# State products in parts of 64 rows and whole 128x128 scores for chunks 0 to 8 of a linear attention with a feed-forward layer

## The chip, the core and the metric

The kernel runs on one core of a Trainium2 chip. The core has a matrix engine (TensorE, in the profile PE, its weight loads PEld), a vector engine (VectorE, DVE), a scalar engine (ScalarE, ACT), a general engine (GpSimd, POOL) and SyncE (SP), which here issues all DMA transfers between the main memory and the on-chip memory (SBUF). TensorE writes its results to PSUM, from which the other engines read. The metric is the device time of one execution in microseconds (us); the figure given for a kernel is the median of several runs.

## The reference

A recurrence with a state of 48x48 for each of 4 batches and 8 heads runs over 768 time steps; its output goes through a token mixing of rank 32 and a feed-forward layer of 384 to 1536 to 384 channels, all in fp32.

```python
def _attn_ref(r, k, v, w, u):
    state = np.zeros((B, H, D, D))
    for t in range(S):
        cur = np.einsum('bhd,bhe->bhde', u[None] * kt, vt)
        y[:, :, t] = np.einsum('bhd,bhde->bhe', rt, state + cur)
        state = wt[:, :, :, None] * state + np.einsum('bhd,bhe->bhde', kt, vt)

def _moe_ref(x, U, V, w_ch1, w_ch2):
    h = x.transpose(0, 2, 1) @ U @ V
    u = x + h.transpose(0, 2, 1)
    return u + np.maximum(u @ w_ch1, 0.0) @ w_ch2
```

## The kernel before

The recurrence is cut into 24 chunks of 128 time steps, six for each batch; chunk g belongs to batch g // 6. Heads stand in pairs: pair j (0 to 3) has its even head in partitions 0 to 47 and its odd head in partitions 64 to 111. Within a chunk the recurrence becomes matrix products. VectorE scans the decays (`scan_f`, L393, and `scan_q`, L408); r and k are scaled by the scans (L416, L421, L423). Then the chunk has these steps on PE:

- the scores (`scores`, L560, step AM): products of scaled k and scaled r over the 48 channels of a head, written to the PSUM tile `aps` of 128 x 2 x 4 x 128. Only k at or before r in time matters. The keys are cut into two halves of 64, and each head's product is made in parts of 64 output rows: one half of the keys meets all 128 times of r, the other only the last 64. The quarter that stays out was set to zero once, at the start (L236). For pairs 2 and 3 the halves of the keys stand in swapped order;
- the u products (`rows_by_u`, L499, step MD, chunks 0 to 5): the diagonal of the scores;
- the transposition of k (`turn_k`, L525, step KT, chunks 0 to 8), which ScalarE copies to the SBUF tile `kn` (`copy_k`, L545, step KN). For chunks 9 to 23 (`TURN_K_DVE`) VectorE and DMA transfers transpose k in blocks of 32 instead;
- the state products (`state_add`, L577 and L578, step DS): kn times v, written to the PSUM tile `dS` in parts of 32 rows. For chunks 1 to 4 (`ADD_Z_PE`) PE also adds the old state Z with a product by the identity matrix (L577) in front of each; for the others VectorE adds it (L608). The last chunk of a batch has no state products;
- y (`y_inner`, L637 and L647, step YA; `y_state`, L660 and L664, step YZ): the scores, merged with the diagonal, times v, and r times the state. Both write parts of 32 rows.

VectorE merges the scores into the tile A that holds the diagonal (`merge`, L567, step CP): a mask says which elements are taken from `aps`. ScalarE makes the next state Z from `dS` (`decay`, L617) and copies y (`out_x`, L681). Behind the chunks come the token mixing and, in seven blocks of time, the feed-forward layer (`ffn`: L888 up, L922 down), whose weights are split into a high and a low half first (L305 to L342).

The order of the work on every engine is written out: the string `ORDER` lists all steps, and `plan` runs them in that order. An engine takes its instructions in that order, and each waits by semaphores for what it reads and for the buffers it writes. SP's queue of transfers is one such list too. [rows N] means the group **Rows N.** below.

Of the kernel before, what the change touches and what calls it, by code (L numbers as in the profile page):

```python
# [13 lines left out]
AF = mybir.ActivationFunctionType  # L14
# [5 lines left out]
B, H, S, D = 4, 8, 768, 48  # L20
P = 128
NP = H // 2
# [14 lines left out]
HP = P // 2  # L37
# [5 lines left out]
TURN_K_DVE, TURN_X_DVE = [9, 10, 11, 12, 13, 14, 15, 16, 17, 18, 19, 20, 21, 22, 23], [9, 10, 11, 12, 13, 14, 15, 16, 17, 18, 19, 20, 21, 22, 23]  # L43
CHOICES = 3
DIAG_PE, LATE_GUARD = [0, 1, 2, 3, 4, 5], []
DIAG_V, MIX_AT_ONCE, X_PE, UP_PARTS = [], [], [], []
LOW_PE = dict(w1=[], w2=[], V=[])
ADD_Z_PE = (1, 2, 3, 4)
W_MAX, W_MAX_BITS, DECAY_MIN = 1.25, 0x3FA00000, 1e-16
HIGH_MIN, HIGH_END = 1.125 * 2.0**-15, 122880.0  # L50
# [108 lines left out]
def rwkv_moe_kernel(ctx, tc, wT, rkT, vN, vS, rkN, uB, uT, uD, U, V, w1, w2, out):  # L159
    nc = tc.nc  # L160
# [18 lines left out]
    def place(kind, shape, name, buf=None, dtype=F32):  # L179

        n = buf.slot if buf else None
        if n is None:
            n = turns[kind] % slots[kind]
            turns[kind] += 1
        return homes.get(kind, sb2).tile(shape, dtype, tag=f"{kind}{n}", name=name)
# [11 lines left out]
    def warm(n, to):  # L197
        for _ in range(n):
            nc.tensor.matmul(to, busy[:, 0:P], busy[:, 0 : to.shape[1]], start=True, stop=True)

    def lead(to):
        if leading[0]:
            warm(leading[0], (to.rearrange("p a b -> p (a b)") if len(to.shape) == 3 else to)[:, 0:TB])

    warm(8, idle)
    ident = const.tile([P, P], F32, name="ident")
# [30 lines left out]
    dS = psS.tile([P, NP, ZW], F32, name="dS")  # L237
# [7 lines left out]
    def step(name, eng, fn, after=(), take=(), use=(), alt=None):  # L245

        s = Step(name, eng, fn, after, list(take), list(use), alt.split() if alt else None)
        steps.append(s)
        return s
# [100 lines left out]
    def chunk(g):  # L350
        b, c = divmod(g, NCH)
        st = sts[g] = dict(buf={p: Buf(p) for p in ("w", "v", "F", "Q", "dv", "kn", "Z", "aps", "y", "dS", "qd")})
        st["buf"].update((p, Buf("big")) for p in ("rk", "kr", "A"))
        buf = st["buf"]
        old = sts.get(g - 1) if c > 0 else None
# [80 lines left out]
        f = step("F " + nm, "DVE", scan_f, [lw], take=[buf["F"]], use=[buf["w"]])  # L436
# [7 lines left out]
        q = step("Q " + nm, "DVE", scan_q, [rc], take=[buf["Q"]], use=[buf["w"], buf["qd"]])  # L444
# [96 lines left out]
                )  # L541

        def copy_k():
            st["kn"] = place("kn", [P, 4, NP, 32], f"kn_{g}", buf["kn"])
            nc.scalar.activation(  # L545
                st["kn"].rearrange("p q j c -> p j q c"), st["trk"].rearrange("p j (q c) -> p j q c", c=32), AF.Copy
            )

        def scores():
            rk = st["rk"]  # L550
            aps = st["aps"] = aps_all
            lead(aps[:, 0])
            for j in range(NQ):
                for h in range(2):
                    for i in range(2):
                        r = slice(64 * i, 64 * i + D)
                        for a in range(2):
                            jj, s0 = j + NQ * (a ^ h), HP * h
                            k0 = HP * a
                            nc.tensor.matmul(  # L560
                                aps[HP * a : HP * a + HP, i, jj, s0:P], rk[r, 1, jj, k0 : k0 + HP], rk[r, 0, jj, s0:P],
                                start=True, stop=True,
                            )
# [4 lines left out]

        def state_add():
            kn, v = st["kn"], st["v"]  # L570
            for j in range(NP):
                for q in range(4):
                    i = q // 2
                    r = slice(32 * q, 32 * q + 32)
                    to = dS[r, j, i * D : i * D + D]
                    if z_pe:
                        nc.tensor.matmul(to, ident[:, r], old["Z"][:, j, i * D : i * D + D], start=True, stop=False)  # L577
                    nc.tensor.matmul(to, kn[:, q, j, :], v[:, j, 64 * i : 64 * i + D], start=not z_pe, stop=True)  # L578

        on = c < NCH - 1  # L580
        z_pe = g in ADD_Z_PE
        if on:
            if g in TURN_K_DVE:
                btk = Buf("big")
                kn = step("KB " + nm, "DVE", turn_k_blocks, [ks], take=[btk], use=[buf["rk"]])
                kn = step("KW " + nm, "SP", send_k, [kn], use=[btk])
                kn = step("KL " + nm, "SP", fetch_k, [kn], take=[buf["kn"]])
            else:
                btr = Buf("ffn")
                kt = step("KT " + nm, "PE", turn_k, [ks], take=[btr], use=[buf["rk"]])  # L590
                kn = step("KN " + nm, "ACT", copy_k, [kt], take=[buf["kn"]], use=[btr])
        am = step("AM " + nm, "PE", scores, [rp, ks], take=[buf["aps"]], use=[buf["rk"]])
        cp = step("CP " + nm, "DVE", merge, [am] + sel_, use=[buf["aps"], buf["A"]])
        if on:
            ds = step(
                "DS " + nm, "PE", state_add, [kn, lv] + ([old["z"]] if z_pe else []), take=[buf["dS"]],
                use=[buf["kn"], buf["v"]] + ([old["buf"]["Z"]] if z_pe else []),
            )
# [651 lines left out]
```

## Time and profile before

| | us |
|---|---|
| median of three runs | 430.25 (428.70 to 431.21) |
| the profiled execution | 429.46 |
| its span, first to last instruction | 427.8 |

Busy time in the span: PE 411.3 us (96%, 4518 matmuls), PEld 359.0 us, DVE 296.6 us (69%), ACT 173.3 us (41%), POOL 121.9 us (28%). The chain that ended last is PE for 82%, 69% of the span in the feed-forward's two lines (35% L922, 34% L888); the scores are 3% of it and the state products 1%. A line of the profile names an engine, a line of the kernel and an operation with its output and inputs; "48*64 48x128" at a matmul means that 48 rows and 64 columns of the array are used and 128 columns move through it (where products of two widths follow each other, the line shows the first). A matmul of fp32 stands as two instructions in the trace.

### The profile page before, as it was taken

To read this page: it belongs to the slowest core of one execution; us is meant where nothing else is said; L and a number is where in the kernel's file an instruction comes from. 1 tells how busy PE (TensorE), PEld (TensorE's weight loads), DVE (VectorE), ACT (ScalarE), POOL (GpSimd) and SP (SyncE) were. 2 spreads that over 40 slices of the span, in tenths; PEclk is the share of its full clock that TensorE was granted. 3 is DMA by queue.
4 is the path that set the end of the run, shared out by engine and by line. 5 is a ranking of instruction groups with operands and counts; after the bars stand their busy time and mean duration, and the time that the engine had idled before them with its cause. 6 is when DMAs were issued, how large, how long until landed. Compare 5 with 4: busy or idle time off the path is not lost.

```text
span 427.8 us, 11110 instructions
## 1 busy us (share of the span) xinstructions
PE 411.3 (96%) x4518; PEld 359.0 (84%) x4518; DVE 296.6 (69%) x585; ACT 173.3 (41%) x499; POOL 121.9 (28%) x164
## 2 busy tenths in 40 slices
PE   6997899999999999999999999999999999999994
PEld 4986668899999898888878888888787899999984
DVE  8999999999879787978749894185851545115610
ACT  5989987768553317645031110351231102100300
POOL 5654656555774530250300201250000010000000
PEclk8569999999999999999999999999999999999998
DMA  8989772476768797656774611425535011001011
GB/s 281 313 289 295 252 272 97 159 227 211 269 221 279 220 302 281 183 170 211 207 231 147 186 58 51 113 89 188 147 103 177 0 61 38 18 5 64 2 38 43
DMA packets 42874, 69.51 MB, mean 163 GB/s; under 512 B 12224, under 2 KB 25280, under 8 KB 42816
## 3 DMA queue, kind: packets, MB, share of 16 engines
q1 hardware_dynamic: 42816, 68.74, 49.9%
q8 instruction: 37, 0.61, 0.6%
q14 instruction: 21, 0.17, 0.1%
HBM read 57.91 MB, written 10.81 MB: 161 GB/s over the span
## 4 chain that ended last, share of the span: by engine, by line
PE 82%; DVE 5%; issue 1%; ACT 0%; POOL 0%; DVEq 0%
PE f L922 35%; PE f L888 34%; PE aps L560 3%; PE y L637 2%; PE y L647 2%; PE y L660 2%; PE dS L578 1%; PE hp L839 1%; PE y L664 1%; PE ga L785 1%; DVE cva_w L318 1%; DVE cva_w L305 1%; PE gb L796 1%; DVE F L393 0%; DVE w1l L342 0%
## 5 line engine op out<-in xcount | busy, mean ns | idle before, releaser
L888 PE MATMUL f<-u,w1h 128*128 128x384 f32 (+1 forms) x504 | 146.8, 363 | 1.0 <-POOL u L855 0.5
L922 PE MATMUL f<-hid,w2h 128*128 128x384 f32 (+1 forms) x504 | 145.8, 363 | 0.9 <-DVE flag L1148 0.9
L888 PEld LDWEIGHTS f<-u,w1h 128*128 128x128 f32 x504 | 92.8, 188 | 12.4 <-issue 1.2
L922 PEld LDWEIGHTS f<-hid,w2h 128*128 128x128 f32 x504 | 92.8, 188 | 10.7 <-issue 2.0
L922 PE MATMUL f<-hid,w2l 128*128 128x384 f32 (+1 forms) x252 | 90.7, 360 | 0.0
L888 PE MATMUL f<-u,w1l 128*128 128x384 f32 (+1 forms) x252 | 90.7, 360 | 0.0
L893 ACT ACTIVATE hid<-f 128x384 fp32r<-128x384 f32 (+1 forms) x50 | 25.9, 527 | 104.8 <-PE f L888 101.8
L899 DVE SCALAR_TENSOR_TENSOR hid<-f,hid 128x384 fp32r<-128x384 f32 (+1 forms) x84 | 50.5, 610 | 23.0 <-ACT hid L893 22.2
L922 PEld LDWEIGHTS f<-hid,w2l 128*128 128x128 f32 x252 | 47.4, 188 | 4.7
L888 PEld LDWEIGHTS f<-u,w1l 128*128 128x128 f32 x252 | 47.4, 188 | 4.1
L472 ACT ACTIVATE A<-ident,dv 128x128 f32<-128x128 f32 x140 | 43.8, 391 | 14.1 <-DVE dv L458 14.0
L940 DVE TENSOR_TENSOR xT<-f,xT 128x384 f32<-128x384 f32 (+1 forms) x21 | 12.6, 607 | 44.0 <-PE f L922 44.0
L855 POOL TENSOR_TENSOR u<-xT,u 128x384 fp32r<-128x384 f32 (+1 forms) x11 | 12.3, 1132 | 90.7 <-DVE u L851 51.9
L567 DVE COPY_PREDICATED A<-maskf,aps 128x1024 f32<-128x1024 uint32 x24 | 31.6, 1315 | 8.4 <-POOL A L478 5.0
L325 POOL TENSOR_TENSOR cva_w<-cva_w,raw_w 128x384 int32<-128x384 int32 x24 | 25.4, 1071 | 36.9 <-ACT raw_w L312 7.2
L408 DVE TENSOR_TENSOR_SCAN Q<-w,starts,qd 128x258 f32<-128x258 f32 x48 | 33.3, 734 | 2.7 <-POOL rk L416 2.2
L416 POOL TENSOR_TENSOR rk<-rk,Q 128x512 f32<-128x512 f32 x15 | 17.9, 1195 | 56.7 <-DVE Q L408 30.7
L393 DVE TENSOR_TENSOR_SCAN F<-w,qd 128x259 f32<-128x259 f32 x48 | 30.4, 676 | 1.3 <-DMA w<-in_wT 1.3
L895 DVE TENSOR_SCALAR hid<-f 128x512 fp32r<-128x512 f32 (+1 forms) x34 | 21.2, 622 | 10.5 <-PE f L888 10.4
L560 PE MATMUL aps<-rk 48*64 48x128 f32 (+1 forms) x768 | 23.5, 265 | 1.4 <-POOL rk L416 1.4
L560 PEld LDWEIGHTS aps<-rk 48*64 48x64 f32 x768 | 20.1, 144 | 5.6 <-issue 2.5
L849 ACT ACTIVATE u<-xT 128x384 fp32r<-128x384 f32 (+1 forms) x15 | 8.1, 563 | 34.8 <-PE f L922 26.0
(126 smaller groups left out, 522.6 us busy)
## 6 DMA issues: line engine op xcount, KB each, us to landing
raw_w<-in_w SPq DMA_DIRECT2D x48, 384.0 KB, 4.6
rk<-in_rkT SPq DMA_DIRECT2D x24, 512.0 KB, 5.5
kr<-in_rkN SPq DMA_DIRECT2D x18, 384.0 KB, 3.8
w<-in_wT SPq DMA_DIRECT2D x24, 260.0 KB, 4.3
v<-in_vS SPq DMA_DIRECT2D x24, 224.0 KB, 4.2
kd<-kt SPq DMA_DIRECT2D x12, 256.0 KB, 3.0
kn<-kd SPq DMA_DIRECT2D x48, 64.0 KB, 3.0
out_dram<-xT SPq DMA_DIRECT2D x12, 192.0 KB, 2.4
```

The source lines that it names most:

```text
L325: lambda: nc.gpsimd.tensor_tensor(out=d["to"].bitcast(I32), in0=d["a"].bitcast(I32), in1=d["e"], op=ALU.add),
L393: nc.vector.tensor_tensor_scan(out=back(F), data0=back(st["w"]), data1=back(qd, OVER * h), initial=1.0, op0=ALU.mult, op1=ALU.add)
L408: nc.vector.tensor_tensor_scan(out=st["Q"][:, a:e], data0=st["w"][:, a:e], data1=qd[:, a - OVER * h : e - OVER * h], initial=starts[:, h : ...
L416: ENG[eng].tensor_tensor(out=rk[:, 0], in0=rk[:, 0], in1=Qv, op=ALU.mult)
L472: nc.scalar.activation(to, one, AF.Copy, scale=dv[:, NP * i + j : NP * i + j + 1])
L560: nc.tensor.matmul(aps[HP * a : HP * a + HP, i, jj, s0:P], rk[r, 1, jj, k0 : k0 + HP], rk[r, 0, jj, s0:P], start=True, stop=True,)
L567: nc.vector.copy_predicated(to, mask2, new)
L888: nc.tensor.matmul(ps, wt[:, f, ct, :], u[ct][:, z], start=(m == 0), stop=(m == 8))
L893: nc.scalar.activation(h[:, 0], d["ps", f], AF.Relu)
L895: nc.vector.tensor_scalar(out=h[:, 0], in0=d["ps", f], scalar1=0.0, scalar2=None, op0=ALU.max)
L899: nc.vector.scalar_tensor_tensor(out=h[:, 1], in0=d["ps", f], scalar=0.0, in1=h[:, 0].bitcast(F32), op0=ALU.max, op1=ALU.subtract)
L922: nc.tensor.matmul(d["o", ct], wt[:, 4 * ct + part, f - 3 * part, :], hid[f][:, z], start=(part == 0 and m == 0), stop=(part == 3 and m == 8),
```

## The change

For chunks 0 to 8 the scores of a head are one product with all 128 keys and all 128 times, so that the masked quarter is computed too; the mask of the merge keeps it out of A. For the same chunks `kn` keeps the layout of the transposition, 128 keys in one piece for each pair, and the state products are made in parts of 64 rows. Where PE adds the old state, the identity products of a pair now all stand in front of its products with v. The steps and their order are the same. Chunks 9 to 23 keep parts of 32 rows and scores in 64 x 128 and 64 x 64.

```diff
+WHOLE_SCORES = range(9)
...
         def copy_k():
-            st["kn"] = place("kn", [P, 4, NP, 32], f"kn_{g}", buf["kn"])
-            nc.scalar.activation(
-                st["kn"].rearrange("p q j c -> p j q c"), st["trk"].rearrange("p j (q c) -> p j q c", c=32), AF.Copy
-            )
+            st["kn"] = place("kn", [P, NP, P], f"kn_{g}", buf["kn"])
+            nc.scalar.activation(st["kn"], st["trk"], AF.Copy)
...
             lead(aps[:, 0])
+            if g in WHOLE_SCORES:
+                for j in range(NP):
+                    for i in range(2):
+                        r = slice(64 * i, 64 * i + D)
+                        nc.tensor.matmul(aps[:, i, j], rk[r, 1, j], rk[r, 0, j], start=True, stop=True)
+                return
...
         def state_add():
             kn, v = st["kn"], st["v"]
+            m = 32 if g in TURN_K_DVE else HP
             for j in range(NP):
-                for q in range(4):
-                    i = q // 2
-                    r = slice(32 * q, 32 * q + 32)
-                    to = dS[r, j, i * D : i * D + D]
-                    if z_pe:
-                        nc.tensor.matmul(to, ident[:, r], old["Z"][:, j, i * D : i * D + D], start=True, stop=False)
-                    nc.tensor.matmul(to, kn[:, q, j, :], v[:, j, 64 * i : 64 * i + D], start=not z_pe, stop=True)
+                parts = [(slice(q, q + m), slice(q // HP * D, q // HP * D + D), q) for q in range(0, P, m)]
+                for r, cs, q in parts if z_pe else ():
+                    nc.tensor.matmul(dS[r, j, cs], ident[:, r], old["Z"][:, j, cs], start=True, stop=False)
+                for r, cs, q in parts:
+                    kq = kn[:, q // 32, j, :] if m == 32 else kn[:, j, r]
+                    vq = v[:, j, 64 * (q // HP) : 64 * (q // HP) + D]
+                    nc.tensor.matmul(dS[r, j, cs], kq, vq, start=not z_pe, stop=True)
```

The rows below list PE's instructions at two places, by line, operation, output, inputs and shape of the output; a number behind a name tells one tile from another, and x8 stands for eight alike. First PE before the change at chunk 8: its state products, its scores, and the token mixing's product behind them.

```order
L578 MATMUL dS<-v_1429,kn_1426 32x48 x16
L560 MATMUL aps<-rk_1023 64x128 x4
L560 MATMUL aps<-rk_1023 64x64 x4
L560 MATMUL aps<-rk_1023 64x128 x4
L560 MATMUL aps<-rk_1023 64x64 x4
L839 MATMUL hp_1_1506<-Vst,gs_1101 128x384
```

The same place on PE after the change (the lines moved by six).

```order
L584 MATMUL dS<-v_1277,kn_1274 64x48 x8
L556 MATMUL aps<-rk_895 128x128 x8
L845 MATMUL hp_1_1338<-Vst,gs_973 128x384
```

Sixteen state products became eight of twice the rows, and sixteen scores of 64 rows became eight of 128 rows, all 128 columns wide; what stands in front and behind is the same.

The second place is PE at the state products of chunk 7 with y of chunk 7 and the transposition of k of chunk 8 behind them, before the change.

```order
L578 MATMUL dS<-v_1055,kn_1227 32x48 x16
L637 MATMUL y_1386<-A_1205,v_1055 32x128 x8
L647 MATMUL y_1386<-A_1205,v_1055 32x128 x8
L660 MATMUL y_1386<-rk_697,Z_1268 32x128 x8
L664 MATMUL y_1386<-rk_697,Z_1268 32x128 x4
L525 MATMUL trk_1415<-ident,rk_1023 128x128 x4
```

And after it.

```order
L584 MATMUL dS<-v_927,kn_1083 64x48 x8
L643 MATMUL y_1234<-A_1061,v_927 32x128 x8
L653 MATMUL y_1234<-A_1061,v_927 32x128 x8
L666 MATMUL y_1234<-rk_625,Z_1124 32x128 x8
L670 MATMUL y_1234<-rk_625,Z_1124 32x128 x4
L526 MATMUL trk_1263<-ident,rk_895 128x128 x4
```

Before, the state products and y had parts of 32 rows alike; now parts of 32 rows follow parts of 64. The products of y are the same.

## Rows read from the trace of the kernel before

**Rows 1.** Stretches: us; busy PE, PEld, DVE, ACT, POOL; PEclk; DMA; GB/s.

```profile
8.10:28.60 20.50, 19.43 (x313) 17.93 (x316) 19.50 (x43) 17.64 (x58) 14.83 (x18) 0.50 0.95 311
28.60:66.30 37.70, 31.80 (x757) 25.36 (x749) 36.33 (x75) 34.12 (x102) 21.31 (x23) 1.00 0.75 260
66.30:100.40 34.10, 33.94 (x374) 31.92 (x374) 33.34 (x70) 25.14 (x70) 19.22 (x20) 1.00 0.54 171
100.40:406.80 306.40, 306.40 (x2985) 267.49 (x2984) 199.07 (x377) 92.70 (x264) 62.46 (x94) 1.00 0.46 146
```

**Rows 2.** Waits of PE from 60 us on: releaser; us in total, times, longest.

```profile
PE f L922 <- DVE flag L1148: 0.9, 1, 0.9
PE f L888 <- POOL u L855: 0.5, 1, 0.5
PE f L888 <- DVE hid L899: 0.3, 1, 0.3
```

**Rows 3.** Chain that ended last, 65.5 to 75 us: start, us, what.

```profile
66.33 6.51 PE f L888 x36
```

**Rows 4.** PE by time, 72 to 80.5 us: start, us, engine, line, count.

```profile
72.78 0.55 PE L578 MATMUL dS<-v,kn 128*32 128x48 f32 x32
73.14 0.62 PE L637 MATMUL y<-A,v 128*32 128x128 f32 x16
73.58 0.62 PE L647 MATMUL y<-A,v 128*32 128x128 f32 x16
...
78.82 0.55 PE L578 MATMUL dS<-v,kn 128*32 128x48 f32 x32
79.29 0.90 PE L560 MATMUL aps<-rk 48*64 48x128 f32 x32
80.12 0.44 PE L839 MATMUL hp<-Vst,gs 96*128 96x384 f32 x1
```

**Rows 5.** PE by time, 35 us: u products of chunk 5, next instruction.

```profile
35.35 0.95 PE L499 MATMUL trd<-u_diag,kr 128*128 128x2 f32 x8
36.23 0.27 PE L577 MATMUL dS<-Z,ident 128*32 128x48 f32 x5
```

**Rows 6.** PE by time, 8 to 12 us: chunk 0.

```profile
8.60 1.56 PE L560 MATMUL aps<-rk 48*64 48x128 f32 x32 [0.95 <-POOL rk L416]
10.09 1.86 PE L499 MATMUL trd<-u_diag,kr 128*128 128x2 f32 x8
11.81 0.45 PE L525 MATMUL trk<-ident,rk 128*128 128x128 f32 x1
```

**Rows 7.** PE by time, 22 to 31 us: chunk 1, u products.

```profile
24.60 0.29 PE L578 MATMUL dS<-v,kn 128*32 128x48 f32 x1 [0.56 <-DMA v<-in_vS]
...
25.73 0.41 PE L637 MATMUL y<-A,v 128*32 128x128 f32 x1
...
28.87 1.05 PE L499 MATMUL trd<-u_diag,kr 128*128 128x2 f32 x8
```

**Rows 8.** PE by time, 38 to 45 us: state products of chunk 4.

```profile
43.32 0.30 PE L577 MATMUL dS<-Z,ident 128*32 128x48 f32 x7 [2.87 <-ACT Z L617]
...
44.24 0.55 PE L754 MATMUL trx<-ident,xT 128*128 128x128 f32 x3
```

**Rows 9.** ScalarE by time, 28 to 31 us.

```profile
29.49 0.48 ACT L681 ACTIVATE xT<-y 128x384 f32<-128x384 f32 x1
```

**Rows 10.** Waits of VectorE, 4 to 66.3 us.

```profile
DVE F L393 <- DMA w<-in_wT: 1.3, 3, 0.5
DVE Q L408 <- POOL rk L416: 0.9, 1, 0.9
```

**Rows 11.** VectorE by time, 25 to 27 us: merge of chunk 2.

```profile
25.49 1.33 DVE L567 COPY_PREDICATED A<-maskf,aps 128x1024 f32<-128x1024 uint32 x1
```

**Rows 12.** ScalarE by line and shape: busy, mean ns, idle before.

```profile
L893 ACT ACTIVATE hid<-f 128x512 fp32r<-128x512 f32 x18 | 10.6, 594 | 39.8 <-PE f L888 39.7
...
L545 ACT ACTIVATE kn<-trk 128x512 f32<-128x512 f32 x8 | 4.6, 578 | 0.0
```

## The prediction

> **What bounds the kernel now.** I read first the table of stretches [rows 1]. Up to 66.3 us PE is not what the kernel waits for: VectorE is busy 19.50 of 20.50 us and then 36.33 of 37.70 us, while PE is busy 31.80 of 37.70 us in the second stretch. From 66.3 us the roles change: PE is busy 33.94 of 34.10 us and then all of 306.40 us. The waits of PE say the same [rows 2]: after 66.3 us it waits once more, 0.9 us at the very end. The chain of waits confirms the border [rows 3]: ahead of 66.33 us it runs through VectorE, behind it through PE. So a microsecond of PE work after 66.3 us is a microsecond of the end, and one before it counts only if it makes VectorE or ScalarE late.
>
> Then I placed the changed products on PE's time line. Nine scores (chunks 0 to 8) and eight state products (0 to 4, 6 to 8) change. Only three of the seventeen stand behind the border: the state products of chunk 7 at 72.78 us and of chunk 8 at 78.82 us, and the scores of chunk 8 at 79.29 us [rows 4]. From chunk 9 on nothing changes on PE. On VectorE, POOL and SP no instruction is added, removed or moved; on ScalarE only the access pattern of eight copies differs.
>
> **What sets the time of these products.** An fp32 product is two matmul instructions in the trace. PE runs products that use different rows and columns of its array side by side; I call the share that one product uses a part, and one instruction on each part a turn. Three prices follow:
> - A turn of 128 moving columns: 16 matmuls of y on four parts, so four turns, take 73.58 - 73.14 = 0.44 us [rows 4], 0.11 us a turn.
> - A turn of 48 moving columns with weights of 32 columns: 32 matmuls on four parts, eight turns, take 73.14 - 72.78 = 0.36 us [rows 4], 0.045 us.
> - A turn that has to load 128 weight columns and moves only two: eight take 36.23 - 35.35 = 0.88 us [rows 5], again 0.11 us. Here nothing but the weights can set it, so I take 0.055 us for 64 weight columns: half, an estimate.
>
> **The change part by part.**
>
> *Scores.* Before, 32 matmuls on four parts: four turns of 128 columns and four of 64, 4 x 0.11 + 4 x 0.055 = 0.66 us. The chunk takes 80.12 - 79.29 = 0.83 us [rows 4], so 0.17 us is start and end. After, 16 matmuls on two parts that each take all 128 columns: eight turns of 128 columns, 0.88 + 0.17 = 1.05 us, **+0.22 us**. The halved count saves nothing, since the parts are halved too, and the masked quarter is what is added. At the low clock (0.50 until 28.6 us [rows 1]) the whole took 10.09 - 8.60 = 1.49 us [rows 6]; there I take 0.44 us more for each of chunks 0 to 2.
>
> *State products without the old state (chunks 0, 6, 7, 8).* Before eight turns on four parts, after eight turns on two. The moving columns stay 48, so the low end is no change. If 64 weight columns set the turn, it is 8 x (0.055 - 0.045) = +0.08 us. I take the second, since [rows 5] shows the weights setting a turn: **+0.16 us** for chunks 7 and 8.
>
> *State products with the old state (1 to 4).* 64 matmuls, 16 turns: chunk 4 takes 44.24 - 43.32 = 0.92 us [rows 8], 0.057 us a turn. After, 16 turns of 0.045 to 0.055 us, so -0.2 to 0 us. At the low clock, chunk 1, it took 25.73 - 24.60 = 1.13 us [rows 7] or 0.07 us a turn; there a turn of 128 weight columns takes (11.81 - 10.09) / 8 = 0.215 us [rows 6], so 64 would take 0.11 us: up to +0.6 us.
>
> *From state products to y.* Both have 32-column weights before, and y follows chunk 7's state products without a gap: 0.36 us. Chunk 8's state products, equally many, are followed by scores with other parts, and take 79.29 - 78.82 = 0.47 us [rows 4]. The 0.11 us more is the price of another division of the array. The change puts it between the state products and y of chunks 1, 2 and 7, and only 7 stands behind the border: **+0.11 us**; the low end is zero. The Trainium skill, "TensorEngine Tiling (Array Packing)", section Key Properties, says that another tiling mode drains the engine first; the trace agrees with 0.47 against 0.36 us, and without that rule the sum would be 0.1 us lower.
>
> *Copies of k.* ScalarE writes k in one piece, where it wrote four blocks: 0.578 us a copy now [rows 12]. The number of elements stays, so I take nothing; a tenth either way, 0.06 us a copy, lies in ScalarE's part of the early stretch and moves the end by less than that.
>
> *What is hidden, and by what.* Before 66.3 us PE gets eight scores and six state products of this. The tightest place that I found: ScalarE's copy of y of chunk 1 at 29.49 us [rows 9], and PE goes on from its last product at 28.87 us [rows 7]: 0.62 us of cover. Ahead of it PE becomes later by 3 x 0.44 + 0.1 + 0.6 + 0.2 = 2.2 us at most, less the 0.56 us that it waits for v anyway [rows 7]: 1.6 us. What is left after 28.6 us runs at the full clock and takes half, so y would end near 29.6 us, 0.1 us too late. Behind ScalarE's copy stand, in its queue, copies of k and the diagonals that VectorE's merges read. With the cover gone it is up to 1.0 us; I take 0. The merge itself is safe: chunk 2's starts at 25.49 us [rows 11], and by 24.60 us PE is past its scores and in the state products [rows 7]. Later PE waits 2.87 us for ScalarE's Z [rows 8], which takes up the rest. VectorE's own waits there are for w and for POOL, none for PE [rows 10].
>
> **Sum.** 0.22 + 0.16 + 0.11 + 0 = +0.49 us, against the profiled execution: 429.46 us (span 427.8 us and 1.7 us around it) becomes 429.95 us. The median of the runs shown is 430.25 us, 0.8 us above that execution; on it the forecast is **430.75 us**, which I give as 430.8. Within 0.5% (2.15 us), which is about what a measurement can tell, that is no change.
>
> **Rivals.**
>
> A, slower: the two row halves of a whole product do not run side by side, because each wants all columns. Then scores have 16 turns: 1.76 + 0.17 = 1.93 us, +1.1 us at the full clock and +2.2 us at the low one. Behind the border +1.1 + 0.27 = 1.4 us. Before it PE is 6.6 us later by chunk 2, y of chunk 1 ends some 2.3 us after 29.49 us, and ScalarE, and behind it VectorE, hand that on: 434.0 us. It decides as soon as the lateness exceeds the 0.62 us of cover. For it: no row shows two parts with 128 weight columns each. Against it: today's scores already run two row halves over the same columns, and reach 0.66 us of turns only so.
>
> B, slower: PE's clock, at 0.50 (1.2 GHz) until 28.6 us and at 1.00 (2.4 GHz) behind [rows 1], rises later, as PE's early work has another shape. Every microsecond of delay costs up to one of PE work, less the cover; 3 us later gives 2.4 + 0.5: 433.2 us. For it: PE was busy 19.43 of 20.50 us at 0.50 and the clock did not rise, so a small difference may decide. Against it: the change gives PE more to do there, not less. An earlier rise gains nothing by itself, since VectorE does not wait for PE there.
>
> C, lower: the time goes with the number of matmuls, which halves. Then scores lose 0.41 us, each state product 0.18 us: 0.8 us behind the border and perhaps 0.5 us ahead of it, 429.0 us. For it: 32 matmuls in 0.83 us are 26 ns each. Against it: 32 in 0.36 us are 11 ns each [rows 4]. The Trainium skill, "TensorE: Matmul & The Clock Gate", section "Wait — 56ns, not 53.3ns?", states that starts never come closer than about 25 ns; the scores' row would fit it, the state products' row contradicts it for parts side by side, so C gets little.
>
> **How the numbers follow.** The forecast, 430.2 to 431.8 us, has 0.70; A 0.08; B 0.07; C 0.10, mostly within the 0.5%; 0.05 is left for a luckier meeting of the early stages by 2 us and more. Slower: A, B and 0.01 of the forecast's tail, 0.16. Faster: 0.02 of C and the 0.05, 0.07. The same: 0.77. The range for eight in ten goes from 428.8 to 433.4 us: C inside, B at its edge, A outside.
>
> **What would show it.** In the new profile the scores of chunk 8 should take about 1.05 us to the next instruction, chunk 7's state products about 0.55 us up to y, and PE should wait for nothing from 66 to about 407 us. Scores of 1.9 us would prove A, of 0.42 us C; a clock that leaves 0.50 later than 28.6 us would be B. If PE's first full-time work starts more than 1 us away from 66.3 us, my claim that the early part hides the change is wrong.

## The result and the profile after

| | before | after |
|---|---|---|
| median of 20 runs each, us | 430.25 | 432.51 |
| the profiled execution, us | 429.46 | 434.35 |
| its span, us | 427.8 | 432.6 |

The changed kernel takes 1.0066 times the time of the kernel before, 95% interval 1.0047 to 1.0085: slower by about 0.7%, and the interval lies wholly above 1. The time lies in the predicted range (428.8 to 433.4 us), but above the 430.2 to 431.8 us of the case that I held likeliest, and what put it there is none of my rivals.

The stretches of the kernel after, cut at the same places of the program; columns as in [rows 1]:

```profile
8.10:28.60 20.50, 18.14 (x222) 16.43 (x222) 20.05 (x45) 17.68 (x59) 15.49 (x18) 0.68 0.97 310
28.60:68.10 39.50, 36.18 (x555) 29.46 (x555) 36.15 (x75) 34.27 (x102) 21.04 (x23) 0.91 0.74 249
68.10:102.58 34.48, 34.26 (x326) 32.55 (x328) 33.60 (x71) 25.28 (x71) 19.39 (x21) 1.00 0.53 166
102.58:411.60 309.02, 306.82 (x2984) 267.59 (x2984) 199.35 (x376) 92.50 (x263) 62.19 (x93) 1.00 0.47 145
```

Three things differ. The border between the early part and the rest stands at 68.1 us, not 66.3. The stretch behind it, with the changed products, is 0.4 us longer. And in the last stretch, where not one product was changed, 309.02 us pass in place of 306.40, and PE is no longer busy in all of them. The waits of PE from 60 us on, against [rows 2], name the place:

```profile
PE y L653 <- issue: 2.2, 1, 2.2
PE f L928 <- DVE flag L1154: 0.9, 1, 0.9
PE f L894 <- DVE hid L905: 0.3, 1, 0.3
PE dS L584 <- DMA kn<-kd: 0.2, 1, 0.2
```

"Issue" means that PE waited for nothing that the profile can name: no engine, no transfer. PE by time shows it in the middle of the products of one y, sixteen alike, of which four run and twelve come 2.2 us later:

```profile
200.44 0.90 PE L565 MATMUL aps<-rk 48*64 48x128 f32 x32
201.26 0.65 PE L643 MATMUL y<-A,v 128*32 128x128 f32 x16
201.72 0.39 PE L653 MATMUL y<-A,v 128*32 128x128 f32 x4
204.31 0.52 PE L653 MATMUL y<-A,v 128*32 128x128 f32 x10 [2.20 <-issue]
```

In the kernel before the same products run through:

```profile
198.24 0.90 PE L560 MATMUL aps<-rk 48*64 48x128 f32 x32
199.07 0.64 PE L637 MATMUL y<-A,v 128*32 128x128 f32 x16
199.53 0.62 PE L647 MATMUL y<-A,v 128*32 128x128 f32 x16
199.97 0.62 PE L660 MATMUL y<-rk,Z 128*32 128x128 f32 x16
```

Last, the changed products behind the border, PE by time in the kernel after, against [rows 4]:

```profile
74.54 0.67 PE L584 MATMUL dS<-v,kn 128*64 128x48 f32 x16
75.14 0.65 PE L643 MATMUL y<-A,v 128*32 128x128 f32 x16
75.60 0.62 PE L653 MATMUL y<-A,v 128*32 128x128 f32 x16
...
80.70 0.67 PE L584 MATMUL dS<-v,kn 128*64 128x48 f32 x16
81.30 1.16 PE L556 MATMUL aps<-rk 48*128 48x128 f32 x16
82.40 0.44 PE L845 MATMUL hp<-Vst,gs 96*128 96x384 f32 x1
```

From start to start, chunk 7's state products take 0.60 us (0.36 before), chunk 8's 0.60 us (0.47) and its scores 1.10 us (0.83).

If each matmul behind 84 us is set against its counterpart in the trace of before, the 4.8 us by which PE's last matmul comes later in the profiled execution of after come apart like this: +1.76 us at the border (66.33 to 68.09), +0.64 us for the three products, -0.52 us for two short waits of before that are gone, +0.30 us at 102 us (0.22 of it the wait for `kn` above), +2.58 us at the stall, 0.04 us elsewhere. The stall costs more than its 2.20 us of idle time, since the matmuls on its two sides no longer overlap.

### The profile page after: what moved, and what is told of

Same layout as the page of the kernel before. It is cut to its first block, busy times and chain, and to the rows that moved or that the text cites. A ratio compares the mean times of both kernels' runs of the same rounds, so it can differ in the third digit from the quotient of the medians.

```text
span 432.6 us, 10438 instructions
## 1 busy us (share of the span) xinstructions
PE 415.1 (96%) x4182; PEld 362.4 (84%) x4182; DVE 297.2 (69%) x585; ACT 173.5 (40%) x499; POOL 121.7 (28%) x164
## 4 chain that ended last, share of the span: by engine, by line
PE 85%; ACT 5%; DMA 4%; DVE 3%; issue 1%; SPq 0%; POOL 0%; DVEq 0%
PE f L928 35%; PE f L894 34%; PE aps L565 3%; PE y L643 2%; ACT A L473 2%; PE y L653 2%; PE y L666 2%; PE dS L584 2%; DMA raw_V<-in_V 1%; DMA kr<-in_rkN 1%; DMA rk<-in_rkT 1%; PE ga L791 1%; PE aps L556 1%; PE hp L845 1%; PE y L670 1%
## 5 line engine op out<-in xcount | busy, mean ns | idle before, releaser
L687 ACT ACTIVATE xT<-y 128x384 f32<-128x384 f32 x24 | 11.6, 481 | 20.3 <-PE y L670 20.3
L433 ACT ACTIVATE junk<-w,b_max 128x512 uint8<-128x512 uint32 x24 | 17.1, 715 | 4.7 <-DMA w<-in_wT 4.6
```

What stands on the lines that cost most here:

```text
L433: nc.scalar.activation(junk, wv.bitcast(U32), AF.Relu, bias=b_max, scale=2.0**-23, accum_out=guard[:, g : g + 1])
```

## The experiments

Each kernel was timed in five rounds against the kernel before on the same chip; ratios are to it. In the expectations, theory F says that what counts is where the borders of instruction packets fall, and theory R that the parts of 64 rows cost the time themselves. The first four kernels ran before F was formed, against a theory 1: the longer scores of chunk 5, which fell into a stretch of low clock (0.50) in the profile of after, make VectorE's merge late.

**Which half of the change costs.** The kernel before, unchanged, as a control:

> The kernel before, unchanged, as a second sample. It shows how its times spread with the granted clock of the early part. If the low clock of the early part is what costs, its executions with a mean clock near 1.00 should be about 2 us shorter than those with 0.97; if the early part hides the clock, both should lie within 1 us of each other. Ratio to the kernel before: 1.000 plus or minus 0.002.

429.50 us, 0.9989 [0.9956, 1.0022]. Its profile holds a surprise: the first full-time product starts at 67.76 us, not at 66.33 [rows 3]. Stretches of it, columns as in [rows 1]:

```profile
43.00:49.40 6.40, 5.00 (x81) 3.87 (x73) 4.54 (x9) 5.20 (x16) 5.80 (x7) 0.50 0.45 122
50.00:60.00 10.00, 9.71 (x203) 6.72 (x203) 8.54 (x19) 7.57 (x21) 3.22 (x3) 1.00 0.98 356
```

And the same of the kernel after:

```profile
43.00:49.40 6.40, 6.28 (x70) 5.26 (x74) 4.69 (x10) 5.77 (x17) 6.40 (x8) 0.50 0.58 197
50.00:60.00 10.00, 9.71 (x173) 6.62 (x167) 8.68 (x18) 7.26 (x20) 3.22 (x3) 1.00 0.99 347
```

The low clock from 43 to 49 us (0.50, so 1.2 GHz) is there without any change, and so is a first full-time product that comes late, by 1.4 us here and by 1.8 us in after. Both belong to an execution, not to a kernel. The chain of this execution runs through PE at that place, through the state products of chunk 4 and the scores of chunk 5, and holds a wait on "issue" too:

```profile
43.19 1.40 issue
...
45.96 1.49 PE aps L560 x32
```

That of after has no such wait there, but the changed scores at the same low clock:

```profile
45.90 2.01 PE aps L556 x16
```

So in these two executions PE's work in the early part is not hidden. In all fourteen profiles of this document the chain runs through PE near 45 us in the seven whose granted clock is 0.50 there, and in none of the seven with 1.00. As to the spread that this run was to show: of the 35 runs of the kernel before that stand beside this one, the 9 with a mean granted clock of 0.99 or more have a median of 428.58 us and the other 26 one of 429.73 us, 1.1 us more, between the two outcomes that I had named.

The whole scores alone:

```diff
+WHOLE_SCORES = range(9)
...
+            if g in WHOLE_SCORES:
+                for j in range(NP):
+                    for i in range(2):
+                        r = slice(64 * i, 64 * i + D)
+                        nc.tensor.matmul(aps[:, i, j], rk[r, 1, j], rk[r, 0, j], start=True, stop=True)
+                return
```

> Whole scores for chunks 0 to 8, state products in parts of 32 rows as before. Theory 1 (the longer scores make VectorE's merge of chunk 5 late, in the stretch behind ScalarE's Z of chunk 3, and 0.26 us of chunk 8's scores come on top): +1.5 to +2.5 us, and in the profile a wait of VectorE's merge for the scores. Theory 2 (the state products and the change to parts of another size in front of y cost the time): at most +0.4 us.

429.59 us, 0.9993 [0.9966, 1.0020], no stall. The state products alone (this edit is against the changed kernel):

```diff
-WHOLE_SCORES = range(9)
+WHOLE_SCORES = []
```

> State products in parts of 64 rows for chunks 0 to 8, scores as before. Theory 1: +0.3 to +0.5 us, which is the 0.37 us by which the state products of chunks 7 and 8 with what follows them grew behind 66 us. Theory 2: +1.5 to +2.5 us.

432.17 us, 1.0062 [1.0037, 1.0087]: all of the loss. None of its 12 runs has a mean clock of 0.99 or more; beside the 26 runs of the kernel before that have none either (429.73 us), the loss is 2.4 us. Its waits of PE from 60 us on begin with a stall at the same place of the program, but in other products (line 643 is the first half of y):

```profile
PE y L643 <- issue: 0.9, 1, 0.9
```

The changed kernel with the old scores in chunk 5:

```diff
-WHOLE_SCORES = range(9)
+WHOLE_SCORES = [0, 1, 2, 3, 4, 6, 7, 8]
```

> The changed kernel with the scores of chunk 5 alone in the old parts. Theory 1: the merge of chunk 5 is on time again, unless PE's clock is low there, so of the 2.3 us about 0.6 to 1.0 us are left. If the lateness gathers over all chunks instead, it stays within 0.4 us of the changed kernel, +1.9 to +2.3 us.

431.90 us, 1.0052 [1.0027, 1.0077]. Its profile has a stall of 0.84 us in the same products, and one wait that no other profile has: 1.1 us at 157.8 us, for VectorE, behind a transfer of `rk` that took 5.95 us. Theory 1 fell: without chunk 5's scores the loss stays, and with all scores but no parts of 64 rows there is none. By these four, theory R looked good.

**Parts of 64 rows, or borders of packets.** The instructions of PE reach it in packets: the page after counts 35 in its section on queues ("q8 instruction: 35, 0.57", so some 16 KB each), that of before 37, for 8462 and 9134 recorded PE instructions. The stalls stand at PE instruction 5057 (after and the one without chunk 5) and 5313 (state products alone): 256 apart, as the whole kernels are not. An fp32 product is four instructions, two matmuls and two weight loads, so each experiment moves the border by a number that can be counted. The next four kernels were built for that. In their edits WHOLE_SCORES lists the chunks with whole scores, and PARTS64 those whose copies of k and state products are made as in the changed kernel. The state products of chunks 1 to 4 in 64 rows, which takes out 256 instructions, one packet:

```diff
+WHOLE_SCORES, PARTS64 = [], [1, 2, 3, 4]
```

> State products in parts of 64 rows for chunks 1 to 4 alone (those with the old state), everything else as before. PE has 256 instructions fewer (128 matmuls and their loads). The profiles so far show PE's instructions coming in packets of 16 KB, some 256 instructions each, and a stall of PE between 200 and 205 us, right at such a packet, in the kernels whose count differs by 384 (parts of 64 alone: 0.9 us), 640 and 672, not in those with 0 and 288. Theory F (what counts is where the borders of these packets fall, so the count modulo 256): 256 is the place of before, no stall near 200 us, ratio 1.000 plus or minus 0.002. Theory R (the parts of 64 rows themselves cost, wherever they stand): two thirds of the 2.7 us of the kernel with all of them, +1.8 us.

429.25 us, 0.9970 [0.9941, 0.9999], no stall. Those of chunks 0, 6, 7 and 8, 128 fewer:

```diff
+WHOLE_SCORES, PARTS64 = [], [0, 6, 7, 8]
```

> State products in parts of 64 rows for chunks 0, 6, 7 and 8 alone. PE has 128 instructions fewer, as far off modulo 256 as 384. Theory F: a stall of about 1 us or more near 200 us and 0.37 us behind chunks 7 and 8, in all +1.4 to +2.7 us, although fewer products are changed than in chunks 1 to 4. Theory R: a third of 2.7 us, +0.9 us, and no stall.

431.31 us, 1.0029 [0.9998, 1.0059], a stall, in its waits of PE:

```profile
PE y L659 <- issue: 1.1, 1, 1.1
```

All state products in 64 rows and the whole scores of chunks 0 to 3, 512 fewer:

```diff
+WHOLE_SCORES, PARTS64 = [0, 1, 2, 3], [0, 1, 2, 3, 4, 6, 7, 8]
```

> All state products of chunks 0 to 8 in parts of 64 rows, and whole scores for chunks 0 to 3. PE has 384 + 128 = 512 instructions fewer, the place of before modulo 256. Theory F: no stall near 200 us, so +0.3 to +0.7 us, though it changes more than the kernel with the parts of 64 rows alone, which has +2.7 us. Theory R: at least +2.5 us.

430.06 us, 1.0004 [0.9978, 1.0031], no stall, with every state product changed. And only the whole scores of chunks 0 to 3, 128 fewer:

```diff
+WHOLE_SCORES, PARTS64 = [0, 1, 2, 3], []
```

> Whole scores for chunks 0 to 3 alone, state products as before. PE has 128 instructions fewer. Theory F: the stall near 200 us, +1 to +2.3 us, though whole scores for all nine chunks cost nothing. Theory R: no change, within 0.5 us.

431.14 us, 1.0016 [0.9986, 1.0047], and a stall of 1.10 us, with no state product changed. The interval of this time includes 1, as that of the kernel with chunks 0, 6, 7 and 8 does, so these two speak by the stall in their profiles and not by their times. R fell here: all state products changed and no loss, none changed and a stall.

**Moving the border by nothing but the start.** PE begins with eight idle matmuls of 512 columns, ahead of any real work. They are bf16, so each is two instructions. Cut into more and shorter ones they move about as many columns and take about as long (3.54 to 3.81 us in the three kernels below, where the eight take 3.59), and the first product behind them starts within 0.1 us of where it starts in the control (5.76 us). The changed kernel again as a control:

> The changed kernel as it is, beside the three that follow. Both theories: 432.5 us against 430.2 for the kernel before, ratio 1.005 to 1.007; PE stands still for 2.2 us between 202 and 204.4 us, and an instruction packet of 16 KB comes 2 to 3 us before it goes on.

432.81 us, 1.0058 [1.0030, 1.0086]; the stall in its profile is 0.94 us this time, and its first full-time product starts at 65.83 us. The chain of this execution:

```profile
65.83 6.51 PE f L894 x36
72.35 0.60 PE dS L584 x16
72.95 0.57 PE y L643 x16
```

The changed kernel with 88 short ones, so that 512 fewer instructions than before are left:

```diff
-    warm(8, idle)
+    for _ in range(88):
+        nc.tensor.matmul(idle[0:32, 0:48], busy[:, 0:32], busy[:, 0:48], start=True, stop=True)
```

> The changed kernel, but the 8 idle matmuls of 512 columns with which PE starts are 88 of 48 columns (as much moved, before PE's first real work): 160 PE instructions more, so that it has 512 fewer than the kernel before, two whole packets. Theory F (what counts is where the borders between packets of 256 instructions fall): no stall near 200 us, only the +0.6 us of the products stays, 430.4 to 431.0 us where the kernel before has 430.2, some 1.6 us below the changed kernel beside it. Theory R (the parts of 64 rows, or the work around them, cost it themselves): no difference from the changed kernel, 432.5 us, stall of about 2 us as there.

430.31 us, 0.9994 [0.9964, 1.0024], beside 432.81 us of the changed kernel: to within the interval the loss is gone, with the change whole. PE by time at the place of the stall:

```profile
199.03 0.90 PE L566 MATMUL aps<-rk 48*64 48x128 f32 x32
199.85 0.65 PE L644 MATMUL y<-A,v 128*32 128x128 f32 x16
200.31 0.62 PE L654 MATMUL y<-A,v 128*32 128x128 f32 x16
200.75 0.62 PE L667 MATMUL y<-rk,Z 128*32 128x128 f32 x16
```

With 136, a whole packet more than the changed kernel, as the control of this edit:

```diff
+    for _ in range(136):
+        nc.tensor.matmul(idle[0:32, 0:32], busy[:, 0:32], busy[:, 0:32], start=True, stop=True)
```

> The same with 136 of 32 columns: 256 PE instructions more than the changed kernel, one whole packet, so every border falls where it fell in the changed kernel, one packet later. Theory F: the stall near 200 us stays, 432.0 to 432.5 us. If short idle matmuls at the start help by themselves (by the clock, say), it is at 430.6 us like the one with 88.

433.06 us, 1.0067 [1.0033, 1.0102], a little more than F expected. The stall is back, after the same four products:

```profile
200.89 0.39 PE L654 MATMUL y<-A,v 128*32 128x128 f32 x4
201.96 0.52 PE L654 MATMUL y<-A,v 128*32 128x128 f32 x10 [0.68 <-issue]
```

The early clock does not explain the difference. Among executions with a mean granted clock of 0.99 or more the medians are 432.54 us for the changed kernel (8 runs), 430.31 us with 88 short ones (8 runs) and 433.02 us with 136 (5 runs).

And the kernel before, with 72, half a packet more:

```diff
+    for _ in range(72):
+        nc.tensor.matmul(idle[0:32, 0:56], busy[:, 0:32], busy[:, 0:56], start=True, stop=True)
```

> The kernel before, no product of it changed, with 72 idle matmuls of 56 columns in place of the 8: 128 PE instructions more, half a packet, as in the kernels that had 128 or 384 fewer and stalled. Theory F: PE stands still for about 1 us near 200 us and the time is about 431.3 us, ratio 1.002 to 1.004. Theory R: no difference from the kernel before, 430.2 us.

431.51 us, 1.0036 [1.0002, 1.0070]: none of its real products is changed, and it stalls:

```profile
199.78 0.41 PE L638 MATMUL y<-A,v 128*32 128x128 f32 x4
201.58 0.52 PE L638 MATMUL y<-A,v 128*32 128x128 f32 x10 [1.39 <-issue]
```

All kernels by the place of the border; "moved by" is the change in PE instructions, taken modulo 256 (-160 is the same place as +96):

| kernel | moved by | remainder | stall in its profile, us | median, us | median before, us |
|---|---|---|---|---|---|
| before, unchanged | 0 | 0 | none | 429.50 | 429.27 |
| 64 rows, chunks 1 to 4 | -256 | 0 | none | 429.25 | 429.91 |
| 64 rows, and scores 0 to 3 | -512 | 0 | none | 430.06 | 429.91 |
| after, 88 short | -512 | 0 | none | 430.31 | 430.01 |
| scores alone | -288 | -32 | none | 429.59 | 429.27 |
| 64 rows, chunks 0, 6 to 8 | -128 | -128 | 1.10 | 431.31 | 429.91 |
| scores 0 to 3 | -128 | -128 | 1.10 | 431.14 | 429.91 |
| before, 72 short | +128 | -128 | 1.39 | 431.51 | 430.01 |
| state products alone | -384 | -128 | 0.95 | 432.17 | 429.27 |
| after, old scores in chunk 5 | -640 | -128 | 0.84 | 431.90 | 429.27 |
| after | -672 | -160 | 2.20 and 0.94 | 432.51, 432.81 | 430.25, 430.01 |
| after, 136 short | -416 | -160 | 0.68 | 433.06 | 430.01 |

The remainder sorts the stalls; what was changed does not. The times follow less closely: at -128 the two kernels with the most changed products (432.17 and 431.90 us) lie above the other three, and whether the products, the clock or longer stalls put them there isn't shown. The best of all, 64 rows in chunks 1 to 4, is 0.3% below the kernel before, at the edge of what can be told, and rests on one group of rounds.

## Why the prediction was right and wrong

**The products: right.** The two row halves of a whole product run side by side: chunk 8's scores take 1.10 us, where I had 1.05, rival A 1.93 and rival C 0.42. From state products to y it is 0.60 us, where I had 0.55. Together the three cost 0.64 us for the 0.49 of the sum. The division of the array, for which I paid 0.11 us once, seems to cost in both state products: each takes 0.60 us, and each is followed by products of another division.

**What they cost at the end: in part taken up by a wait that I overlooked.** "A microsecond of PE work after 66.3 us is a microsecond of the end" was too strict. In [rows 2] I looked at PE's matmuls alone. The waits of the weight loads in the kernel before, from 79 to 84.5 us, have one more:

```profile
PEld f L888 <- DVE xT L844: 0.4, 1, 0.4
```

Behind the products of chunk 8 PE waited for VectorE, and since the matmul in front was still draining, only 0.12 us of that were idle time of PE; from start to start the two matmuls there stand 0.46 us apart, where 0.17 is usual. In the profile of after this wait, and a shorter one of 0.13 us at 77 us, are gone: VectorE comes 1.89 us later than in before, PE 2.28 us, so the longer products fill the gap. The kernels with the border at its old place fit that: 1.0004 with all state products and four scores, 0.9994 with the whole change. But among executions with a mean clock of 0.99 or more the whole change stands at 430.31 us (8 runs) and the kernel before in the same rounds at 429.17 us (9 runs). What is left lies between nothing and 1.1 us, and no run narrows it further.

**The early part: right at the full clock, not at the low one.** I had named a first full-time product more than 1 us away from 66.3 us as proof against me. It came at 68.09 us, but also at 67.76 us in the kernel before unchanged, with the same low clock, and at 65.83 us in a second profile of the changed kernel, at the full clock. The sign was too tight for what one execution differs from the next. Where the clock is at 0.50 near 45 us, though, the changed products are not hidden: the scores of chunk 5 take 2.01 us on the chain, for 1.49 us unchanged. The 2.87 us that PE waits for Z, which I let take up the rest, lie in front of chunk 4's state products and of these scores, and cover neither. Rival B goes the same way: the clock did stay low later, and it does so without the change. I had 0.16 for a loss of more than 0.5%, nearly all of it for A and B. That the median fell into the range for eight in ten is therefore luck: the top of the range was there for B, and what filled it is a term that my sum did not have.

**From chunk 9 on: wrong, and this is the step that failed.** "From chunk 9 on nothing changes on PE" holds for the list of instructions, the only thing I compared. It does not hold for how they reach PE, and for that the sum had no term; between the changed kernel and the same with 88 short idle matmuls it is 2.5 us. The change takes 672 instructions out of PE's list, all in front of 84 us; so every border between packets of 256 falls elsewhere in what follows. Counted from the first recorded one, all eight stalls behind 60 us that the profiles name "issue" stand at instruction 5057, 5313, 5569 or 5825, which are multiples of 256 apart: at a border. And each ends 2.3 to 2.5 us after a packet began to arrive (201.83 to 204.31 us in after, 198.15 to 200.65 in its second profile, 199.16 to 201.58 in the kernel before with 72 short ones). The queue of these packets in after from 201.7 to 202 us (from 198.5 to 201.7 us it has none), and in before from 194.3 to 195 us:

```profile
q8 instruction: 1, 0.02, 19.7%
q8 instruction: 1, 0.02, 10.6%
```

If packets are given to borders in order, no border in the fourteen profiles is crossed sooner than 2.2 us after its packet began to arrive, and the kernels that do not stall near 200 us cross theirs 2.7 to 3.2 us after it (in before 194.50 and 197.26 us). The early part has five such stalls more, of 0.5 to 3.5 us, at instruction 961, 1217 or 1473, the same steps. One is the 1.40 us of the kernel before unchanged, whose other profile crosses that border without a wait: the kernel before is not free of them, and where they come changes with the execution too.

Why there, of all places behind 60 us: in a stretch of f a packet lasts PE up to 29 us (232.5 to 261.8 us in after), but near 200 us the state products, scores and y of two chunks stand close together, in small products that run side by side. In after the packet before the stall starts at 198.56 us and is used up at 202.1; the next began to arrive at 201.8 only. In before, the border falls ahead of these products, at 194.38 us, and the packet begins to arrive at 194.5. These times show a border that waits for its packet; that PE holds no more than the packet it works off and the one behind it is my reading of them. The Trainium skill, "Runtime: NRT & Kernel Launch", section "Instruction fetch mechanics", says that instructions are fetched in blocks of 16 KiB, 256 of them, and that the cost of crossing a border is mostly hidden; the traces agree with the block, and with "mostly": of the 27 borders behind 60 us in after, one has a wait on "issue".

**What stays open.** Why the packet for the next border begins 0.1 us behind a border at one place (194.38 us in before), 3.3 us at another (198.56 us in after), and elsewhere up to 3.9 us ahead of it (328.1 us in after): the DMA engines are busy to 0.83 of the time from 196 to 200 us in after, and to 0.87 in before, which explains no difference. And the size: the stalls in the profiles (0.7 to 2.2 us) are partly shorter than the difference of the medians (432.81 less 430.31, so 2.5 us, between the changed kernel and the one with 88 short matmuls in the same rounds). How long they are in the timed runs no trace shows.

## What to carry to other kernels

Where PE never waits, count its instructions as well as their time: taking some out in one place moves the borders of instruction packets in all that follows, and a border in a dense run of small products can cost more than the edit. A wait on "issue" in an unchanged stretch is the sign, and more but shorter idle matmuls at the start, which change little but the count, tested it here and mended it. Take more than one profile of each kernel: two of the same kernel differed here by a stall, and by 1.4 us in where the first full-time product starts. Look for waits on the weight loads too before you say that the path has no slack.

## What the runs showed of the hardware

- A border of 256 PE instructions held PE for 0.68 to 2.20 us in eight profiles, in the middle of a row of products that depend on nothing new; PE went on 2.3 to 2.5 us after the packet began to arrive.
- Two profiles of one unchanged kernel differ in this: at instruction 1473 one waits 1.40 us, the other not at all.
- With 48 moving columns in fp32 a turn takes about 0.058 us with weights of 64 columns (16 matmuls on two parts, eight turns, in 0.60 us with some 0.13 us of start and end), where it took 0.045 us with weights of 32; with weights of 128 columns and two moving columns it takes 0.11 us [rows 5].
